# A planner that starts with its queue and two engines taken: one core, windowed attention into a softplus feed-forward

## The chip, the core and the metric

One core of one Trainium2 chip runs the kernel. The metric is the device time of one execution in microseconds (us). TensorE (PE) multiplies and loads its weights beside that (PEld), VectorE (DVE), ScalarE (ACT) and GpSimd (POOL) work on elements, SyncE (SP) issues the transfers, and the DMA engines carry them.

## The reference, cut to what matters

```python
scores = scale * np.matmul(q, k.transpose(0, 1, 3, 2))        # 8 x 8 heads, 576 x 64
mask_plain = (rel >= 0) & (rel < 32)                          # heads 0 to 3
mask_dil = (rel >= 0) & (rel < 128) & (rel % 4 == 0)          # heads 4 to 7
scores = np.where(masks, scores, -1e9)
attn = np.exp(scores - scores.max(-1))
attn = attn / (attn.sum(-1) + 1e-9)
x = np.matmul(attn, v)                                        # then 4608 tokens x 512
h = x @ w_in                                                  # 512 x 2048
g = np.maximum(h, 0.0) + np.log1p(np.exp(-np.abs(h)))
out = g @ w_out                                               # 2048 x 512
```

## The kernel before

The 4608 tokens are nine chunks of 512. All products are carried in high and low parts, so each product of a weight block is three matmuls of 512 columns (`xh`, `xl` and `parts`, `gh`, `gl`). Chunks 0 to 2 use the plain products: `h_ps` and `o_ps` are their sums in PSUM. Chunks 3 to 8 go in three pairs (`SUPERS`) through a scheme with seven products of sums of blocks instead of eight; its sums in PSUM are `x`, `y`, `z`, and `unit()` issues the matmuls of one product block. The sums of weight blocks that it needs (`w_b`, `w_t`) are worked out on DVE, ACT and POOL while the first chunks run, stored to DRAM (`keep_block` and `job`, 256 KB each) and fetched later into a ring of five buffers (`ring`).

Attention goes by couples of head groups. For each couple there are two "visits" of TensorE, which stand between the long matmuls: `scores` (`s_ps`) and `values` (`a_ps`). Behind the scores come the maximum and the exponentials, then `turn_squares`, a transpose on DVE that writes `sq`; four `turned<-sq` transfers of 64 KB write it to DRAM, and one `sq<-turned` of 256 KB fetches it back in the order that `values` needs. The values visit has two halves, one for each group of the couple (`a_ps<-v,sq` and `a_ps<-x_full,sq`), and each waits for a fetch of `sq`. Its results are normalized, turned, sent out (`rows<-x_full`) and fetched back (`x_full<-rows`) as the chunk's x.

All these transfers are issued by SP through `load_dma`, in one order. Each of the first 128 waits until the eighth before it has landed, so at most eight are under way.

What comes in which order is set in two ways. The start, up to about 98 us, is written out by hand (the string `OPENING`). All the rest is a list of tasks with costs and due times, which `planned()` puts in order when the kernel is built: for each engine it keeps when it is free, for the queue `queue_free`, and it takes the most urgent task that can begin. TensorE's own chain has a fixed order; only the visits are put in by the planner. `HURRIED` changes the urgency of tasks by their number, `CHOSEN` pins a task to one engine. The core of the planner is

```python
start = min(b for b, _ in begins)
if e == "SP":
    start = max(start, queue_free - BACKLOG)
_, at, n, t = min((not t.visit, urgency(t), t.n, t) for b, t in begins if b <= start)
...
if t.size:
    queue_free = max(queue_free, end) + t.size / DMA_RATE
    end = queue_free + DMA_LATENCY + t.size * DMA_EACH
```

At the end, `o_after()` adds the last sums of product 6 to `temp` and stores the last tiles (`out_t<-g_of`).

Of the kernel before, what the change touches and what calls it, by code (L numbers as in the profile page):

```python
# [18 lines left out]
ALU = mybir.AluOpType  # L19
# [5 lines left out]
P = 128  # L25
# [3 lines left out]
CH = 512  # L29
# [18 lines left out]
HALF = CH // 2  # L48
# [8 lines left out]
DEPTH = 8  # L57
THIN = 128
LAG = 2
HURRIED = {  # L60
# [6 lines left out]
}  # L67
CHOSEN = {
    295: "ACT", 467: "DVE", 535: "DVE", 554: "DVE", 586: "DVE", 595: "DVE", 819: "DVE", 853: "DVE", 865: "DVE",
    868: "DVE", 882: "DVE", 885: "DVE", 888: "DVE", 901: "DVE", 903: "DVE", 905: "ACT", 908: "DVE", 1210: "DVE",  # L70
    1213: "DVE", 1219: "DVE", 1238: "DVE", 1266: "DVE", 1281: "DVE", 1307: "DVE", 1322: "DVE", 1336: "DVE",
    1345: "DVE", 1580: "DVE", 1670: "DVE", 1676: "DVE", 1694: "DVE", 1716: "DVE", 1731: "DVE", 1767: "DVE",
    1772: "DVE", 1777: "DVE", 2010: "DVE", 2042: "DVE", 2094: "DVE", 2112: "DVE",
}
EXP_AND_LN = [t.name for t in act_sets.SETS].index("natural_log_exp_and_others")

# [38 lines left out]
def tile_windowed_attention_softplus_ffn(  # L115
# [47 lines left out]
    def load_dma(engine=None, **kw):  # L163
        ins = tc.keep_in_program_order((engine or nc.sync).dma_start(**kw))
        if held[0] is not None:
            tc.add_manual_dep(
                ins.ins,
                held[0].ins.name,
                mybir.DependencyInfo(mybir.DependencyClass.Sync, mybir.DependencyReason.DATA),
                reason="the load is held back until this matmul",  # L170
            )
            held[0] = None
        if engine is None and len(under_way) < THIN:
            if len(under_way) >= DEPTH:
                tc.add_manual_dep(
                    ins.ins,
                    under_way[-DEPTH].ins.name,
                    mybir.DependencyInfo(mybir.DependencyClass.Sync, mybir.DependencyReason.DATA),
                    reason="at most so many of the first loads under way",
                )  # L180
            under_way.append(ins)
# [740 lines left out]
    def transfer(run, *what, size, n=1, each=0.4, reads=(), writes=()):  # L922
        return Task("SP", each * n, lambda: run(*what), reads, writes, size=size)
# [52 lines left out]
    TILE = 2 * P * CH * 4  # L976
# [263 lines left out]
    BANKS = "xzyxyzy"  # L1240
# [8 lines left out]
    def bank_of(b, j):  # L1249
        if (b, j) not in banks:  # L1250
            n = "xyz".index(b)
            banks[b, j] = bank(f"{b}_{j}", "h" if b == "x" else f"o{2 * (n - 1) + j}")
        return banks[b, j]
# [16 lines left out]
    def unit(u):  # L1270
        _, i, k, jj = units[u]
        x, b = PRODUCTS[k][0], BANKS[k]
        begins = k < 3
        w = ring[u % RING]
        for n in range(2):
            dst, m = bank_of(b, n), 0
            for kk in range(2):
                for wp, xp in ((0, 0), (0, 1), (1, 0)):
                    if i == 0:
                        lhs, rhs = w[:, n, wp, kk * P : (kk + 1) * P], blocks[x][xp][:, kk]  # L1280
                        first, final = begins and m == 0, m == 5
                    else:
                        lhs, rhs = w[:, kk, wp, n * P : (n + 1) * P], moving[u % 3][xp][:, kk]
                        first, final = begins and jj == 0 and m == 0, jj == NCP - 1 and m == 5
                    matmul(out=dst, lhsT=lhs, rhs=rhs, start=first, stop=final, skip_group_check=not begins)
                    m += 1

    def evicted(k, j, dst, keys, t):
        b = BANKS[k]
        key = BANK_KEY[b][j]  # L1290
        if t is None:
            copy_task("ACT", 512, lambda: (dst()[:, j], banks[b, j]), reads=[key], writes=keys)
            return
        task(
            "DVE", 512, lambda: summed("DVE", dst()[:, j], banks[b, j], temps[t][:, j], ALU.add),
            reads=[key, (f"t{t}", j)], writes=keys,
        )
# [83 lines left out]
    def o_after(s, k):  # L1381
        first, second = SUPERS[s]
        to, t = ((0, None), (1, 0), (2, 0), ("a11", None), ("a22", 1), ("a12", 2), ("a21", 0))[k]
        if k == 3:
            half, c = 0, first
            n = next(turn_of_e) % 2
            keys, dst = both(f"e{n}"), lambda: spare[n]
        elif k > 3:
            half, c = ((1, second), (1, first), (0, second))[k - 4]
            name = {4: "a21", 5: "a11", 6: "a12"}[k]  # L1390
            keys, dst = g_keys(name, 1), lambda: g[name, 1]
        else:
            keys, dst = both(f"t{to}"), lambda: temps[to]
        for j in range(2):
            evicted(k, j, dst, [keys[j]], t)
            if k == 6 and s == len(SUPERS) - 1:
                rows = slice(j * P, (j + 1) * P)
                transfer(
                    lambda rows=rows, j=j: load_dma(out=out[rows, c * CH : (c + 1) * CH], in_=dst()[:, j]),
                    reads=[keys[j]], size=TILE // 2,  # L1400
                )
        if k > 2 and not (k == 6 and s == len(SUPERS) - 1):
            transfer(store, dst, half, c, reads=keys, size=TILE)

# [66 lines left out]
    def planned():  # L1471
        engines = ("PE", "POOL", "DVE", "ACT", "SP", "NONE")
        free, candidates = dict.fromkeys(engines, 0.0), {e: [] for e in engines}
        queue_free = port_free = seen = 0.0
        for t in reversed(tasks):
            for other in t.then:
                t.latest = min(t.latest, other.latest - t.tail())

        def offered(t):
            for e in t.options:  # L1480
                candidates[e].append(t)

        for t in tasks:
            if not t.left:
                offered(t)
        for _ in tasks:
            best = None
            for e in engines:
                begins = [
                    (max(free[e], t.ready, port_free if e in t.ports else 0.0, seen + APART if t.visit else 0.0), t)  # L1490
                    for t in candidates[e]
                ]
                if not begins:
                    continue
# [4 lines that stand above are left out]
                if best is None or (start, at, n) < best[:3]:  # L1499
                    best = start, at, n, t, e  # L1500
            start, _, _, t, e = best
            for other in t.options:
                candidates[other].remove(t)
            t.engine, t.begun, end = e, start, start + t.options[e]
            free[e] = end
            if t.visit:
                seen = end
            if e in t.ports:
                port_free = end
# [3 lines that stand above are left out]
            yield t  # L1513
            for other in t.then:
                lag = (
                    0.0 if e == other.main == "PE" else calm(other, end) if other.visit else 0.5 if other.main == "PE"
                    else 0.12 if other.main == e else 0.18
                )
                other.ready = max(other.ready, end + lag)
                other.left -= 1  # L1520
                if not other.left:
                    offered(other)
# [133 lines left out]
```

## Time and profile before

| | |
|---|---|
| Median of 3 runs | 817.3 us (816.92 to 817.5) |
| Profiled execution, device time | 819.88 us |
| Its span on the core | 818.1 us |
| TensorE busy | 801.9 us, 98% |
| DVE, ACT, POOL busy | 660.2, 501.8, 189.4 us |
| Moved by DMA | 218.94 MB, mean 268 GB/s |

The span is the time from the first to the last instruction on the core; the device time of the same execution is 1.8 us more. The profiled execution is 2.6 us over the median of the runs. Of the page's forty slices, TensorE's granted clock is below 0.9 in one alone, the second (0.6).

### The profile page before, as it was taken

The numbers are of one execution on the slowest core, as the hardware profiler recorded it, in microseconds if no ns is written. First come the engines' busy times: TensorE is split into PE (matmuls) and PEld (weight loads), VectorE is DVE, ScalarE is ACT, GpSimd is POOL, SyncE is SP. The second block draws the span as 40 slices with busy tenths as digits, with TensorE's granted clock in tenths as the row PEclk, the third lists the DMA queues.
The fourth block names the chain that finished last, engine by engine and source line by source line (L and its number), as shares of the span: only waits on it lengthen the run. The fifth ranks groups of instructions, "written<-read, shape, count | busy, mean of one in ns | idle before, by whom it ended". The sixth has DMA issues, their size and how long they took to land.

```text
span 818.1 us, 19668 instructions
## 1 busy us (share of the span) xinstructions
PE 801.9 (98%) x7833; PEld 654.2 (80%) x7835; DVE 660.2 (81%) x967; ACT 501.8 (61%) x1122; POOL 189.4 (23%) x132
## 2 busy tenths in 40 slices
PE   6999999999999999999999999999999999999998
PEld 4678888788888888888787888888888888888886
DVE  4798899957687766897999887897997846778974
ACT  5787788745666645596786413889943616775410
POOL 0000000054043324754313202202024302221510
PEclk9699999999999999999999999999999999999999
DMA  9774999968879673999988999879989675556573
GB/s 298 242 242 129 307 374 339 314 208 287 278 249 296 210 219 142 374 336 357 350 295 303 316 352 333 289 240 346 298 269 308 233 248 189 196 190 199 189 218 140
DMA packets 118490, 218.94 MB, mean 268 GB/s; under 512 B 11520, under 2 KB 53632, under 8 KB 118400
## 3 DMA queue, kind: packets, MB, share of 16 engines
q1 hardware_dynamic: 117968, 216.97, 79.1%
q8 instruction: 62, 1.02, 0.5%
q10 hardware_dynamic: 432, 0.72, 0.3%
q14 instruction: 28, 0.23, 0.1%
HBM read 162.07 MB, written 55.57 MB: 266 GB/s over the span
## 4 chain that ended last, share of the span: by engine, by line
PE 72%; DVE 10%; DMA 9%; ACT 5%; issue 2%; POOL 1%; SPq 0%; POOLq 0%; DVEq 0%; ACTq 0%
PE y L237 20%; PE z L237 12%; PE x L237 12%; PE h_ps L237 11%; PE o_ps L237 10%; PE a_ps L237 3%; DMA raw<-w 3%; PE s_ps L237 3%; DMA w_t<-cast 2%; ACT s L433 2%; ACT e L1308 1%; DVE g_of L940 1%; DVE a L216 1%; DMA v<-vp 1%; DMA k<-kdl 1%
## 5 line engine op out<-in xcount | busy, mean ns | idle before, releaser
L940 POOL TENSOR_TENSOR g_of<-g_of 128x1024 f32<-128x1024 f32 x33 | 80.3, 2434 | 258.6 <-DVE g_of L1311 133.3
L940 DVE TENSOR_TENSOR g<-g_of,g 128x1024 fp32r<-128x1024 f32 x84 | 121.3, 1450 | 15.0 <-ACT g L972 14.5
L237 PE MATMUL o_ps<-gh,parts 128*128 128x512 f32 x384 | 129.2, 394 | 0.0
L237 PE MATMUL h_ps<-xh,parts 128*128 128x512 f32 x384 | 129.1, 394 | 0.0
L972 ACT CAST g<-g_of 128x1024 fp32r<-128x1024 f32 x61 | 63.9, 1051 | 102.8 <-PE z L237 44.3
L1308 ACT ACTIVATE e<-e 128x1024 f32<-128x1024 f32 x96 | 101.1, 1058 | 1.7
L237 PE MATMUL y<-g,ring 128*128 128x512 f32 x432 | 100.5, 390 | 0.0
L237 PEld LDWEIGHTS y<-g,ring 128*128 128x128 f32 x432 | 80.8, 188 | 17.1
L940 POOL TENSOR_TENSOR b<-parts 128x512 f32<-128x512 f32 x29 | 40.4, 1393 | 213.5 <-DVE parts L231 143.8
L237 PEld LDWEIGHTS h_ps<-xh,parts 128*128 128x128 f32 x384 | 72.4, 188 | 15.6 <-DVE x_full L587 0.4
L237 PEld LDWEIGHTS o_ps<-gh,parts 128*128 128x128 f32 x384 | 72.1, 188 | 15.9
L433 ACT ACTIVATE s<-s,nm 128x64 f32<-128x64 f32 x224 | 74.8, 336 | 7.2 <-DVE nm L424 7.1
L237 PE MATMUL h_ps<-xl,parts 128*128 128x512 f32 x192 | 75.0, 391 | 0.0
L237 PE MATMUL o_ps<-gl,parts 128*128 128x512 f32 x192 | 74.8, 390 | 0.0
L237 PE MATMUL z<-g,ring 128*128 128x512 f32 x288 | 66.7, 390 | 0.5 <-DVE g L940 0.5
L237 PE MATMUL x<-g,ring 128*128 128x512 f32 x288 | 66.5, 390 | 0.0
L237 PE MATMUL z<-s_h,ring 128*128 128x512 f32 x192 | 63.3, 390 | 0.7 <-DVE temp L940 0.7
L237 PE MATMUL y<-s_h,ring 128*128 128x512 f32 x192 | 63.6, 392 | 0.3 <-DVE temp L940 0.3
L237 PEld LDWEIGHTS z<-g,ring 128*128 128x128 f32 x288 | 53.9, 188 | 12.1 <-DVE g L940 0.9
L237 PE MATMUL x<-a_h,ring 128*128 128x512 f32 x192 | 63.3, 390 | 0.0
L237 PEld LDWEIGHTS x<-g,ring 128*128 128x128 f32 x288 | 53.9, 188 | 11.5 <-DVE g L940 0.2
L940 DVE TENSOR_TENSOR g_of<-y,temp 128x512 f32<-128x512 f32 x60 | 39.6, 682 | 28.7 <-PE y L237 28.6
(111 smaller groups left out, 1522.4 us busy)
## 6 DMA issues: line engine op xcount, KB each, us to landing
ring<-w_t SPq DMA_DIRECT2D x96, 512.0 KB, 4.7
ring<-w_b SPq DMA_DIRECT2D x72, 512.0 KB, 5.1
raw<-w SPq DMA_DIRECT2D x64, 256.0 KB, 5.6
w_t<-cast SPq DMA_DIRECT2D x64, 256.0 KB, 5.5
w_b<-parts SPq DMA_DIRECT2D x48, 256.0 KB, 5.1
v<-vp SPq DMA_DIRECT2D x14, 512.0 KB, 5.7
x_full<-vp SPq DMA_DIRECT2D x14, 512.0 KB, 5.8
turned<-sq SPq DMA_DIRECT2D x112, 64.0 KB, 3.2
```

Of the source, the lines that this page charges most:

```text
L216: pin(nc.vector.scalar_tensor_tensor(out=ai, in0=low, scalar=29, in1=ai, op0=ALU.logical_shift_right, op1=ALU.bitwise_or,))
L237: last_matmul[0] = tc.keep_in_program_order(nc.tensor.matmul(**kw))
L433: pin(nc.scalar.activation(out=self.blocks[:, t], in_=src, func=AF.Exp, bias=self.nm[:, t : t + 1], scale=1.0 / 8.0 if self.masked else 1. ...
L940: pin((nc.gpsimd if name == "POOL" else nc.vector).tensor_tensor(out=dst, in0=a, in1=b, op=op))
L972: pin(nc.scalar.copy(out=dst, in_=src))
L1308: pin(nc.scalar.activation(out=to(), in_=of(), func=func, **kw))
```

## The change

The planner no longer starts from zero: the queue counts as taken for 14.5 us, DVE for 1.4 and ACT for 1.0, by what the opening left running. The tables `HURRIED` and `CHOSEN` are replaced by others that fit this. In the last unit of all, the matmuls of the second bank are done in two halves of 256 columns, and `o_after()` adds and stores that bank's tile in two halves.

```diff
+BEGUN = {"DVE": 1.4, "ACT": 1.0}
+QUEUE_BEGUN = 14.5
 HURRIED = {
-    18: -46, 57: -2, 80: 8, 81: -22, 173: -2, 179: -36, 180: -16, 183: 28, 198: -30, 295: 30, 338: -16, 554: -4,
...
+    0: -6, 7: 2, 20: -72, 24: -32, 40: -92, 50: -44, 57: -144, 63: -4, 65: -30, 76: -8, 86: -12, 93: -30,
...
-        for n in range(2):
-            dst, m = bank_of(b, n), 0
+        whole = [(n, slice(0, CH)) for n in range(2)]
+        for n, cols in whole if u < len(units) - 1 else [whole[0], (1, slice(0, HALF)), (1, slice(HALF, CH))]:
+            dst, m = bank_of(b, n)[:, cols], 0
...
-                        lhs, rhs = w[:, kk, wp, n * P : (n + 1) * P], moving[u % 3][xp][:, kk]
+                        lhs, rhs = w[:, kk, wp, n * P : (n + 1) * P], moving[u % 3][xp][:, kk, cols]
...
-            evicted(k, j, dst, [keys[j]], t)
             if k == 6 and s == len(SUPERS) - 1:
                 rows = slice(j * P, (j + 1) * P)
-                transfer(
-                    lambda rows=rows, j=j: load_dma(out=out[rows, c * CH : (c + 1) * CH], in_=dst()[:, j]),
-                    reads=[keys[j]], size=TILE // 2,
-                )
+                for n, cols in enumerate((slice(0, CH),) if j == 0 else (slice(0, HALF), slice(HALF, CH))):
+                    width = cols.stop - cols.start
+                    task(
+                        "DVE", width, lambda j=j, cols=cols: summed(
+                            "DVE", dst()[:, j, cols], banks[BANKS[k], j][:, cols], temps[t][:, j, cols], ALU.add
+                        ),
+                        reads=[BANK_KEY[BANKS[k]][j], (f"t{t}", j)], writes=[("last", j, n)],
+                    )
...
     def planned():
         engines = ("PE", "POOL", "DVE", "ACT", "SP", "NONE")
         free, candidates = dict.fromkeys(engines, 0.0), {e: [] for e in engines}
-        queue_free = port_free = seen = 0.0
+        free |= BEGUN
+        queue_free, port_free, seen = QUEUE_BEGUN, BEGUN["DVE"], 0.0
```

The opening's instructions stay as they are, and so does the order of the long matmuls. From about 98 us on, the order on all engines is another. DVE has 990 instructions instead of 967, ACT 839 instead of 837 (by the program's count), POOL 108 instead of 132, SP 718 transfers instead of 717. In the changed file the lines stand 13 further on (L237 becomes L250).

On SP, the first planned stretch, around the first two fetches of `sq`. Before, 35 blocks `w_b` stand between SP's first planned transfer and the first `turned<-sq`, and the piece around the fetches is

```order
L164 DMA w_b_3_1510<-parts 128x2x256
L164 DMA w_b_3_1522<-parts 128x2x256
L164 DMA x_full<-vp 128x1024
L164 DMA turned<-sq 32x4x128 x8
L164 DMA k<-kpl 128x544 x2
L164 DMA mask<-msk 128x512
L164 DMA w_b_3_1530<-parts 128x2x256
L164 DMA w_b_2_1537<-parts 128x2x256
L164 DMA sq<-turned 128x512
L164 DMA w_b_2_1549<-parts 128x2x256
L164 DMA w_b_2_1557<-parts 128x2x256
L164 DMA sq<-turned 128x512
```

and now, with 17 blocks ahead of the first `turned<-sq`,

```order
L177 DMA w_b_0_1547<-parts 128x2x256
L177 DMA turned<-sq 32x4x128 x4
L177 DMA x_full<-vp 128x1024
L177 DMA turned<-sq 32x4x128 x4
L177 DMA k<-kpl 128x544 x2
L177 DMA mask<-msk 128x512
L177 DMA w_b_2_1509<-parts 128x2x256
L177 DMA sq<-turned 128x512
L177 DMA w_b_2_1521<-parts 128x2x256
L177 DMA w_b_2_1529<-parts 128x2x256
L177 DMA w_b_0_1555<-parts 128x2x256
L177 DMA sq<-turned 128x512
```

Ahead of the second fetch stand 39 blocks `w_b` before and 21 now; the other transfers ahead of it are the same. Behind it, before the next couple's fetches, there are now 16 blocks `w_b` in a row, then `turned<-sq` x8, `kept`, two `w_b`, `v`, `rows` x4, `kept` and both fetches of `sq`.

On TensorE, the first planned values visit (`a_ps`). Before, it stands behind 530 long matmuls of 512 columns of the plain chunks:

```order
L237 MATMUL h_ps<-xh,parts 128x512
L237 MATMUL o_ps_2211<-gh,parts 128x512
L237 MATMUL o_ps_2211<-gl,parts 128x512
L237 MATMUL o_ps_2211<-gh,parts 128x512
L237 MATMUL a_ps<-v,sq 32x64 x32
L237 MATMUL a_ps<-x_full,sq 32x64 x32
L237 MATMUL o_ps_2220<-gh,parts 128x512
```

and now behind 458:

```order
L250 MATMUL h_ps<-xh,parts 128x512
L250 MATMUL o_ps_1400<-gh,parts 128x512
L250 MATMUL o_ps_1400<-gl,parts 128x512
L250 MATMUL o_ps_1400<-gh,parts 128x512
L250 MATMUL a_ps<-v,sq 32x64 x32
L250 MATMUL a_ps<-x_full,sq 32x64 x32
L250 MATMUL o_ps_1414<-gh,parts 128x512
```

The visit moves 72 long matmuls forward, the next values visit from 623 to 539 of them, so that 81 lie between the two instead of 93.

On DVE, the place that the kernel before reaches at about 400 us (`cast<-d` finishes a block for `w_t`; the additions into `temp` read the banks of `y` and `z` and so free them for TensorE). Before:

```order
L1311 SCALAR_TENSOR_TENSOR g_of<-g_of,e 128x1024
L1120 TENSOR_TENSOR cast<-d,cast 128x2x256
L940 TENSOR_TENSOR temp<-y_4589,temp 128x512
L940 TENSOR_TENSOR temp<-y_4596,temp 128x512
L940 TENSOR_TENSOR temp<-z_4568,temp 128x512
L419 SCALAR_TENSOR_TENSOR s<-s_ps,mask 128x512
L424 TENSOR_REDUCE nm<-s 128x8
L974 CAST g<-g_of 128x1024
L940 TENSOR_TENSOR temp<-z_4561,temp 128x512
```

Now:

```order
L1133 TENSOR_TENSOR cast<-b,cast 128x2x256
L1133 TENSOR_TENSOR cast<-d,cast 128x2x256
L953 TENSOR_TENSOR temp<-z_4566,temp 128x512
L953 TENSOR_TENSOR temp<-z_4573,temp 128x512
L953 TENSOR_TENSOR temp<-y_4590,temp 128x512
L953 TENSOR_TENSOR temp<-y_4597,temp 128x512
L987 CAST g<-g_of 128x1024
```

The two additions for `z` have come ahead of the two for `y`.

## Rows read from the trace of the kernel before

**Rows 1.** The page: engine table, and one group of weight loads (busy us, mean ns)
```profile
PE 801.9 (98%) x7833; PEld 654.2 (80%) x7835; DVE 660.2 (81%) x967; ACT 501.8 (61%) x1122; POOL 189.4 (23%) x132
...
L237 PEld LDWEIGHTS y<-g,ring 128*128 128x128 f32 x432 | 80.8, 188 | 17.1
```

**Rows 2.** TensorE's waits from 100 us on: total us, times, longest
```profile
PE a_ps L237 <- DVE a L207: 1.4, 1, 1.4
PE z L237 <- DVE temp L940: 0.7, 1, 0.7
PE z L237 <- DVE g L940: 0.5, 1, 0.5
PE y L237 <- DVE temp L940: 0.3, 1, 0.3
```

**Rows 3.** Timeline of TensorE around two values visits: start, duration, instruction, [idle before]
```profile
156.18 0.85 PE L237 MATMUL a_ps<-v,sq 64*32 64x64 f32 x64 [1.40 <-DVE a L207]
156.83 0.85 PE L237 MATMUL a_ps<-x_full,sq 64*32 64x64 f32 x64
157.60 0.50 PE L237 MATMUL o_ps<-gh,parts 128*128 128x512 f32 x1
157.94 0.39 PE L237 MATMUL o_ps<-gl,parts 128*128 128x512 f32 x1
...
178.61 0.39 PE L237 MATMUL h_ps<-xh,parts 128*128 128x512 f32 x1
178.93 0.80 PE L237 MATMUL a_ps<-v,sq 64*32 64x64 f32 x60
```

**Rows 4.** Timeline of SP's transfers, 109.8 to 152.4 us: start, us until the last issue
```profile
109.92 1.02 SPq L164 DMA_DIRECT2D x_full<-qp  x2
...
112.14 9.59 SPq L164 DMA_DIRECT2D w_b<-parts  x12
...
123.22 18.48 SPq L164 DMA_DIRECT2D w_b<-parts  x23
...
142.55 4.39 SPq L164 DMA_DIRECT2D turned<-sq  x8
...
151.85 0.51 SPq L164 DMA_DIRECT2D sq<-turned  x1
```

**Rows 5.** Windows: busy us of each engine, PEclk, DMA share, GB/s
```profile
114.40:156.10 41.70, 40.38 (x299) 32.99 (x297) 41.46 (x81) 34.91 (x95) 1.42 (x1) 1.00 1.00 335
110.00:128.00 18.00, 18.00 (x81) 14.92 (x80) 17.93 (x35) 16.25 (x41) 0.00 (x0) 1.00 1.04 363
128.00:147.00 19.00, 19.00 (x206) 15.62 (x205) 18.97 (x39) 16.08 (x40) 0.00 (x0) 1.00 0.99 325
157.00:179.00 22.00, 22.00 (x167) 17.97 (x161) 15.70 (x25) 12.84 (x34) 10.35 (x11) 1.00 0.85 267
...
380.00:410.00 30.00, 28.98 (x305) 23.04 (x306) 26.24 (x43) 20.97 (x42) 11.59 (x9) 1.00 1.00 352
```

**Rows 6.** Timeline of DVE, 128 to 143 us: the first `sq` transpose
```profile
132.34 0.66 DVE L475 STREAM_TRANSPOSE sq<-s 128x512 f32<-128x512 f32 x1
```

**Rows 7.** Timeline of ACT, 395 to 404 us
```profile
400.71 0.62 ACT L972 CAST cast<-d 128x512 fp32r<-128x512 f32 x1 [1.64 <-DMA w_t<-cast]
```

**Rows 8.** Timeline of DVE, 396 to 408 us
```profile
401.98 1.28 DVE L940 TENSOR_TENSOR temp<-y,temp 128x512 f32<-128x512 f32 x2
```

**Rows 9.** Timeline of TensorE, 400 to 410 us
```profile
402.71 0.50 PE L237 MATMUL y<-s_h,ring 128*128 128x512 f32 x1 [0.32 <-DVE temp L940]
...
406.43 0.50 PE L237 MATMUL z<-s_h,ring 128*128 128x512 f32 x1 [0.70 <-DVE temp L940]
```

**Rows 10.** Timeline of all engines, 805 to 819 us: the last addition
```profile
814.20 0.69 DVE L940 TENSOR_TENSOR g_of<-y,temp 128x512 f32<-128x512 f32 x1 [0.67 <-PE y L237]
```

**Rows 11.** DVE by line and form: an operation on 256 columns (busy us, mean ns)
```profile
L620 DVE TENSOR_TENSOR xl<-a_ps,xh 128x256 fp32r<-128x256 f32 x8 | 3.0, 417 | 0.7 <-ACT xh L616 0.7
```

**Rows 12.** Timeline of TensorE, 44 to 45 us: four transposes of 128 columns
```profile
44.48 0.60 PE L464 MATMUL t_ps<-opened,s 128*128 128x128 f32 x4
```

More of the change, by code (lines that the diff above doesn't have):

```diff
@@ L59 @@
 LAG = 2
+BEGUN = {"DVE": 1.4, "ACT": 1.0}
+QUEUE_BEGUN = 14.5
 HURRIED = {
[6 rows of a table removed]
[14 rows of a table added]
 }
 CHOSEN = {
[L69 to L73, printed above, removed]
+    285: "DVE", 292: "ACT", 314: "DVE", 323: "DVE", 324: "DVE", 325: "DVE", 326: "DVE", 535: "DVE", 536: "DVE",
+    537: "DVE", 544: "DVE", 560: "DVE", 564: "DVE", 577: "DVE", 593: "DVE", 594: "DVE", 595: "DVE", 796: "ACT",
+    819: "DVE", 822: "DVE", 827: "DVE", 829: "DVE", 852: "DVE", 853: "DVE", 871: "DVE", 873: "DVE", 875: "DVE",
+    882: "DVE", 883: "DVE", 885: "DVE", 898: "DVE", 901: "DVE", 903: "DVE", 908: "DVE", 1079: "ACT",
+    1210: "DVE", 1216: "DVE", 1224: "DVE", 1266: "DVE", 1281: "DVE", 1292: "ACT", 1296: "ACT", 1307: "DVE",
+    1312: "DVE", 1322: "DVE", 1335: "DVE", 1345: "DVE", 1584: "ACT", 1625: "DVE", 1670: "DVE", 1731: "DVE",
+    1741: "DVE", 1748: "DVE", 1772: "DVE", 1777: "DVE", 1782: "DVE", 1783: "ACT", 1790: "DVE", 1795: "DVE",
+    1800: "DVE", 1805: "DVE", 2010: "DVE", 2034: "DVE", 2063: "DVE", 2104: "DVE",
 }
@@ L1394, in o_after @@
         for j in range(2):
-            evicted(k, j, dst, [keys[j]], t)
             if k == 6 and s == len(SUPERS) - 1:
                 rows = slice(j * P, (j + 1) * P)
-                transfer(
-                    lambda rows=rows, j=j: load_dma(out=out[rows, c * CH : (c + 1) * CH], in_=dst()[:, j]),
-                    reads=[keys[j]], size=TILE // 2,
-                )
+                for n, cols in enumerate((slice(0, CH),) if j == 0 else (slice(0, HALF), slice(HALF, CH))):
[6 more added lines that the diff above has]
+                    )
+                    transfer(
+                        lambda rows=rows, j=j, cols=cols: load_dma(
+                            out=out[rows, c * CH + cols.start : c * CH + cols.stop], in_=dst()[:, j, cols]
+                        ),
+                        reads=[("last", j, n)], size=width * P * 4,
+                    )
+                continue
+            evicted(k, j, dst, [keys[j]], t)
         if k > 2 and not (k == 6 and s == len(SUPERS) - 1):
```

18 rows, old and new, of the table HURRIED are left out of this document.

## The prediction

> **What bounds the kernel now.** I read the page's engine table first. TensorE is busy for 801.9 us of a span of 818.1 us [rows 1], so almost nothing can be won except where it stands idle, and everything that makes it stand costs the full time. The profiled execution took 819.88 us, 2.6 us more than the median of the three runs (817.3 us). The sum below is made on its trace and then added to the median.
>
> The list of TensorE's waits from 100 us on is next [rows 2]. The opening, up to about 98 us, is issued as before, so its waits stay. Behind it are only four: 1.40 us before an `a_ps` visit, and 0.3, 0.7 and 0.5 us before `y` and `z`. Together they are 2.9 us: this is all that a better order can win, apart from the last few microseconds of the kernel.
>
> The largest one must be understood. The timeline of TensorE [rows 3] shows a values visit that starts at 156.18 after 1.40 us of nothing. The row puts the wait down to a DVE instruction `a` that has no link to the visit. The program makes the visit wait for its two `sq` fetches, and the second of these was issued by SP at 151.85 [rows 4], 4.33 us before the visit started. For a transfer of 256 KB in a full queue that is what one expects, so I take the fetch for the cause. And why was it issued so late? SP's timeline shows one unbroken row of issues: twelve `w_b` blocks took 9.59 us, the next 23 took 18.48 us, which is 0.80 us a block both times. The windows [rows 5] say why: over 114.4 to 156.1 us the DMA engines were busy for a share of 1.00 at 335 GB/s. **SP's place in line is the clock of this stretch: what stands ahead of a fetch decides when it lands.** The `sq` transposes which feed it ran at 132.34 and soon after [rows 6], ten microseconds before SP came to `turned<-sq` at 142.55.
>
> The Trainium skill, "DMA: Bandwidth & Descriptors", section "Specifications", gives about 358 GB/s as the limit of HBM for one core. The rows of this case (335 over the whole stretch, 363 at best) agree.
>
> **The change, part by part.**
>
> *The first values visit.* Two things move, and they move by different amounts. On TensorE the visit stands after 458 of the long 512-column matmuls instead of 530, so 72 fewer. Such matmuls follow each other by 0.227 us: from the one at 157.94 to the one at 178.61 [rows 3] there are 91 steps in 20.67 us. 72 of them are 16.35 us, so TensorE is at the visit at 154.78 - 16.35 = 138.43 us (154.78 is the start less the wait of 1.40). Its second half starts 0.65 us behind the first (156.18 to 156.83), which is 139.08. On SP the second `sq` fetch has 21 `w_b` blocks ahead of it from 109.9 us on, instead of 39; all other transfers ahead of it are the same ones (two `k` loads, two of queries, two of `v`, eight `turned`, two more of `k`, a mask, the first `sq`). So it is issued 18 x 0.803 = 14.45 us earlier, at 137.40, and its data are there 4.33 us later, at 141.73. TensorE gains 16.35 us on its place and the queue only 14.45. The second half waits 141.73 - 139.08 = **2.65 us**, and the old 1.40 us go. Bounds: at 363 GB/s, the fastest window [rows 5], the 27.5 us from 109.92 to 137.40 would shrink in the ratio 335/363 to 25.4, and the wait to 0.5; if the queue stays at 317 to 325 GB/s, as it did where `turned` was written, it grows to about 3.5.
>
> *The second values visit* (the other couple of the same chunk). Between the two visits TensorE has 81 long matmuls, where it had 93. From the start of the second half of the first visit it is there after 0.77 (156.83 to 157.60) + 0.34 + 80 x 0.227 + 0.32 us = 19.6, at 161.3. SP carries, behind the second `sq` of the first couple and up to the first `sq` of this one: 18 `w_b`, eight `turned` of a quarter block, two `kept`, a `v` of two blocks, four `rows` of half a block, and that `sq`: 27 blocks of 256 KB. At 0.803 us they take 21.7, to 163.4. So it waits **2.1 us**. The second estimate comes from the old chain: from 157.60, where the first visit ended, to 178.93, where the second began with its data just there, are 21.33 us; the same chain from 142.50 ends at 163.8 and gives 2.5. That chain was not held by the queue alone, since the window 157 to 179 shows only 267 GB/s, and so the wait can also be 0. I take 2.1 and keep 0 to 2.5.
>
> *Around 400 us.* The queue is full again (352 GB/s, share 1.00 [rows 5]). ACT's `cast<-d` waited 1.64 us for a store of `w_t` [rows 7], DVE came to the additions into `temp` only at 401.98 [rows 8], and TensorE waited 0.32 for `y` and 0.70 for `z` [rows 9]. In the new order the four additions behind that `cast<-d` are `z`, `z`, `y`, `y` instead of `y`, `y`, `z`, and then the other `z` after three more rows. Thus `y` comes two additions later, about 1.2 us (a pair took 1.28 from the start of one to the end of the other [rows 8], and they overlap a little), and the wait for `z` disappears: +1.2 - 0.7 = +0.5. Half of it I strike off, as the block itself may be earlier by a little: **+0.2**, bounds -1.5 (all three waits gone) and +1.5.
>
> *The end.* The last addition (DVE 814.20, 0.69 us [rows 10]) becomes two of 256 columns, 0.42 each [rows 11], the first of which lies beside the matmuls. That takes off 0.27. The last store has half the bytes; I give that nothing to 0.3. The six last matmuls become twelve of 256 columns. Their number of columns is the same. Weight loads double to twelve at 188 ns [rows 1], 2.26 us if one could not begin before the last had ended, against 1.36 us of matmuls: that would cost 0.9. But four transposes of 128 columns, each with a weight load of its own, took 0.60 us together [rows 12], less than four such loads in a row (0.75), so loads overlap and the halves cost about 0.05 to 0.1. SP issues one more store, but a smaller one. Sum of the end: **-0.3**, bounds -0.6 and +0.7.
>
> *Everything else*: the other visits stay within 12 to 70 long matmuls of their old places and none of them waited before; POOL gets 24 instructions less and DVE 23 more, in stretches where DVE's work lies beside TensorE's. I set them at nothing. If DVE becomes late, the additions that free `y` and `z` are next to be waited for.
>
> Sum: -1.40 + 2.65 + 2.1 + 0.2 - 0.3 = +3.25 us. The profiled execution would take 823.1, the median **820.5 us**.
>
> **The rivals.**
>
> *The queue keeps up.* If the new mix of transfers runs 10% faster than 335 GB/s, both fetches land in time: 24.7 us instead of 27.5 for the first. The old 1.40 goes and the end gives 0.3: 815.6 us, and 814.1 if the waits around 400 go as well (they hang on the same queue). For it: 363 GB/s in 110 to 128 us. Against it: that pace held for 18 us only, and 325 followed with a share of 0.99. The Trainium skill, "DMA: Bandwidth & Descriptors", section "Bandwidth", measured 425 GB/s at 16 MB; at that figure the queue would be ahead of TensorE everywhere, and no window here has shown it for a single stretch. Chance 0.15.
>
> *The waits only change places.* The first visit waits 1.0 to 1.5 us instead of 1.40, and the second finds its data there, because its chain is shorter by the `w_b` and `x_full` transfers that stood between its two fetches. That is 817.0 with the end's gain. For it: the lower bounds above, both reached by a queue only 5% faster. Chance 0.16.
>
> *The blocks themselves are late.* DVE was busy 17.93 of 18 us and 18.97 of 19 [rows 5] while it decodes weights; if the earlier visits' softmax pushes the blocks back, SP, which issues in order, stands at a `w_b` that isn't ready, and the `sq` fetch behind it with it. Three DVE instructions late (0.6 us each) at both places are some 3 us more: 823.5. It decides as soon as SP shows a wait on DVE ahead of the first `turned`. Chance 0.12.
>
> *The halves cost.* Weight loads that do not overlap: 820.5 + 0.3 + 0.7 = 821.5. Chance 0.02.
>
> **How the numbers follow.** The forecast has 0.55, with a range of its own from 818.9 to 822.5. 0.2% is 1.6 us, about what a measurement of this kernel can tell from no change. Faster: the first rival and a little of the second, 0.17. Same: most of the second and the lower edge of the forecast, 0.15. Slower: the rest, 0.68. The range that should hold 8 in 10 takes the forecast, the second rival and the nearer part of the first and the third: 815.4 to 823.4.
>
> **What would show it.** Right: TensorE idle in the middle of the first visit near 139 to 142 us, and before the second near 161 to 164, each ended by an `sq` fetch; SP without a gap and the DMA share at 0.97 to 1.00 there; a wait for `y` near 406 and none for `z`. Wrong: both visits start without a wait; or SP idle in 110 to 140 with a wait on DVE. The end is right if the last DVE row has about 0.42 us and the span ends less than 3.9 us behind the start of the last addition (now 818.1 - 814.2). What would upset the sum most is a queue that moves `w_b` blocks in under 0.75 us.

## The result, and the profile after

The changed kernel takes 824.23 us (median of 6, 823.2 to 825.97) against 817.11 us for the kernel before (median of 6): a ratio of 1.0086, 95% interval 1.0066 to 1.0107, which is +7.0 us (5.4 to 8.7). Slower, as forecast, but by twice as much: the forecast was 820.5, its range ended at 823.4.

TensorE's waits from 98 us on in the profile after (total us, times, longest):

```profile
PE a_ps L250 <- issue: 2.4, 1, 2.4
PE a_ps L250 <- DMA sq<-turned: 2.4, 2, 1.8
PE y L250 <- DVE temp L953: 2.3, 1, 2.3
PE o_ps L250 <- issue: 0.5, 1, 0.5
PE s_ps L250 <- issue: 0.3, 1, 0.3
```

There were 2.9 us of them [rows 2], now there are 7.9. The timeline of TensorE shows where they stand around the first two planned values visits:

```profile
136.32 0.39 PE L250 MATMUL o_ps<-gh,parts 128*128 128x512 f32 x1
137.26 0.85 PE L250 MATMUL a_ps<-v,sq 64*32 64x64 f32 x64 [0.54 <-DMA sq<-turned]
139.96 0.85 PE L250 MATMUL a_ps<-x_full,sq 64*32 64x64 f32 x64 [1.85 <-DMA sq<-turned]
...
142.20 0.40 PE L250 MATMUL o_ps<-gh,parts 128*128 128x512 f32 x1 [0.50 <-issue]
...
159.70 0.39 PE L250 MATMUL o_ps<-gh,parts 128*128 128x512 f32 x1
162.53 1.12 PE L250 MATMUL a_ps<-v,sq 64*32 64x64 f32 x61 [2.44 <-issue]
...
164.50 0.79 PE L250 MATMUL h_ps<-xh,parts 128*128 128x512 f32 x1
165.09 0.63 PE L250 MATMUL h_ps<-xl,parts 128*128 128x512 f32 x1
165.52 0.72 PE L250 MATMUL h_ps<-xh,parts 128*128 128x512 f32 x2
```

The first visit waits in both halves, the second before its start: the places of the forecast. The row of the second names no releaser (`issue`), but it is the fetch too: the first couple's second fetch, issued at 134.56, took 5.3 us to land, and its half starts at 139.96; the next couple's first fetch was issued at 158.62, took 3.8 us, and the second visit starts at 162.53. Behind the second wait something stands that the forecast did not have: the halves of the visit take 1.12 us where one took 0.80 [rows 3], and the next long matmuls start 0.59 and 0.43 us apart instead of 0.34 and 0.227. The windows (busy us of each engine, PEclk, DMA share, GB/s) say why: the granted clock is at the lower of its two levels, 1.2 GHz, for some 3 us.

```profile
160.00:162.50 2.50, 0.09 (x1) 0.01 (x1) 2.50 (x6) 2.34 (x4) 0.00 (x0) 0.96 1.06 335
162.50:163.50 1.00, 0.97 (x73) 1.00 (x77) 0.57 (x1) 0.00 (x0) 0.95 (x1) 0.50 0.99 152
163.50:165.00 1.50, 1.50 (x79) 1.33 (x64) 0.39 (x1) 0.00 (x0) 0.70 (x1) 0.50 0.75 253
165.00:166.00 1.00, 1.00 (x4) 0.77 (x3) 1.00 (x3) 0.00 (x0) 0.00 (x0) 0.64 1.04 384
...
114.40:156.10 41.70, 38.80 (x413) 31.62 (x412) 37.99 (x78) 33.96 (x94) 0.00 (x0) 1.00 1.00 332
```

The last of these rows answers to the first of [rows 5]: 332 GB/s at a share of 1.00, so the queue is as full as before. SP's timeline (start, us until the last issue) answers to [rows 4]:

```profile
107.77 1.00 SPq L177 DMA_DIRECT2D k<-kdl  x2
...
111.92 13.19 SPq L177 DMA_DIRECT2D w_b<-parts  x17
125.20 2.33 SPq L177 DMA_DIRECT2D turned<-sq  x4
...
134.56 1.05 SPq L177 DMA_DIRECT2D sq<-turned  x1
135.65 12.31 SPq L177 DMA_DIRECT2D w_b<-parts  x16
148.09 4.55 SPq L177 DMA_DIRECT2D turned<-sq  x8
```

From SP's first planned transfer to the second fetch are 26.8 us (forecast: 27.5, from 109.92 to 137.40). The third place is near 406 us; the rows are those of ACT, DVE and TensorE, one view each:

```profile
405.50 0.62 ACT L985 CAST cast<-d 128x512 fp32r<-128x512 f32 x1 [3.99 <-DMA w_t<-cast]
```

```profile
406.15 0.69 DVE L1133 TENSOR_TENSOR cast<-d,cast 128x512 fp32r<-128x512 f32 x1 [3.42 <-ACT cast L985]
406.76 1.28 DVE L953 TENSOR_TENSOR temp<-z,temp 128x512 f32<-128x512 f32 x2
407.96 1.28 DVE L953 TENSOR_TENSOR temp<-y,temp 128x512 f32<-128x512 f32 x2
```

```profile
408.69 0.50 PE L250 MATMUL y<-s_h,ring 128*128 128x512 f32 x1 [2.31 <-DVE temp L953]
```

ACT waits for the store of `w_t` for 3.99 us (1.64 in [rows 7]), DVE for ACT, TensorE for DVE. And the end, all engines:

```profile
817.13 0.69 DVE L953 TENSOR_TENSOR g_of<-y,temp 128x512 f32<-128x512 f32 x1 [4.49 <-PE y L250]
818.56 0.76 DVE L953 TENSOR_TENSOR g_of<-y,temp 128x256 f32<-128x256 f32 x2 [0.74 <-PE y L250]
```

Both halves of the last addition stand behind the last matmul, which starts at 818.24; none lies beside it.

The two spans differ by 4.1 us only (822.2 and 818.1), for the openings of the two executions differ as well, with the same instructions: over 16 to 33 us the granted clock was 0.51 in the profile before and 0.90 in the one after. The first planned scores visit starts at 101.73 before and at 100.00 after; from there to the last matmul's start are 712.05 and 718.24 us. So **the planned part became 6.2 us longer**; this is the number to explain. (Up to the start of the last addition but one, which the halves don't touch, it is 6.0 us; up to the end of the span 5.8, as the span ends 4.0 us behind the last matmul's start instead of 4.3.) The clock of the opening alone does not set when it ends: two of the kernels below, the one with the last bank whole and the one with the first visit alone later, had 0.70 over the same stretch and came to that visit at 99.67 and at 101.10.

### The profile page after: what moved, and what is told of

It reads as the page before. It is cut to its first block, busy times and chain, and to the rows that moved or that the text cites. A ratio compares the mean times of both kernels' runs of the same rounds, so it can differ in the third digit from the quotient of the medians.

```text
span 822.2 us, 19653 instructions
## 1 busy us (share of the span) xinstructions
PE 798.2 (97%) x7839; PEld 652.3 (79%) x7841; DVE 662.7 (81%) x990; ACT 501.4 (61%) x1124; POOL 152.3 (19%) x108
## 4 chain that ended last, share of the span: by engine, by line
PE 91%; DMA 5%; DVE 1%; issue 1%; ACT 1%; SPq 0%; POOL 0%; DVEq 0%; ACTq 0%; POOLq 0%
PE y L250 23%; PE o_ps L250 16%; PE z L250 15%; PE x L250 15%; PE h_ps L250 15%; PE a_ps L250 3%; PE s_ps L250 3%; DMA raw<-w 2%; DMA w_t<-cast 2%; DMA k<-kdl 1%; DMA sq<-turned 1%; DMA x_full<-vp 0%; SPq L177 0%; PE t_ps L477 0%; DVE temp L953 0%
## 5 line engine op out<-in xcount | busy, mean ns | idle before, releaser
L250 PE MATMUL o_ps<-gh,parts 128*128 128x512 f32 x384 | 129.3, 394 | 0.5 <-issue 0.5
L250 PE MATMUL h_ps<-xh,parts 128*128 128x512 f32 x384 | 129.5, 395 | 0.0
L985 ACT CAST g<-g_of 128x1024 fp32r<-128x1024 f32 x57 | 59.6, 1049 | 114.6 <-PE y L250 41.0
L953 DVE TENSOR_TENSOR g<-g_of,g 128x1024 fp32r<-128x1024 f32 x84 | 115.1, 1374 | 17.1 <-ACT g L985 16.6
L953 POOL TENSOR_TENSOR g_of<-g_of 128x1024 f32<-128x1024 f32 x26 | 63.4, 2438 | 219.8 <-DVE g_of L1325 112.3
L250 PE MATMUL y<-g,ring 128*128 128x512 f32 (+1 forms) x438 | 100.4, 387 | 0.0
L250 PEld LDWEIGHTS y<-g,ring 128*128 128x128 f32 x438 | 81.3, 188 | 16.9
L250 PEld LDWEIGHTS h_ps<-xh,parts 128*128 128x128 f32 x384 | 72.7, 189 | 15.5 <-DVE e L702 0.2
L250 PEld LDWEIGHTS o_ps<-gh,parts 128*128 128x128 f32 x384 | 72.1, 188 | 15.8
L250 PE MATMUL h_ps<-xl,parts 128*128 128x512 f32 x192 | 75.3, 392 | 0.0
L250 PE MATMUL o_ps<-gl,parts 128*128 128x512 f32 x192 | 74.8, 390 | 0.0
L953 POOL TENSOR_TENSOR b<-parts 128x512 f32<-128x512 f32 x21 | 29.6, 1413 | 231.1 <-DVE parts L244 157.5
L250 PE MATMUL x<-g,ring 128*128 128x512 f32 x288 | 66.8, 391 | 0.0
L250 PE MATMUL z<-g,ring 128*128 128x512 f32 x288 | 66.6, 390 | 0.0
L250 PE MATMUL y<-s_h,ring 128*128 128x512 f32 x192 | 63.5, 392 | 2.3 <-DVE temp L953 2.3
L250 PE MATMUL x<-a_h,ring 128*128 128x512 f32 x192 | 63.3, 391 | 0.0
L250 PE MATMUL z<-s_h,ring 128*128 128x512 f32 x192 | 63.3, 391 | 0.0
L250 PEld LDWEIGHTS x<-g,ring 128*128 128x128 f32 x288 | 53.8, 188 | 11.7 <-DVE g L953 0.3
L953 DVE TENSOR_TENSOR g_of<-y,temp 128x512 f32<-128x512 f32 (+1 forms) x61 | 39.8, 672 | 28.8 <-PE y L250 28.8
L250 PEld LDWEIGHTS z<-g,ring 128*128 128x128 f32 x288 | 54.0, 188 | 11.2
```

The lines of the kernel that those rows point to most:

```text
L250: last_matmul[0] = tc.keep_in_program_order(nc.tensor.matmul(**kw))
L953: pin((nc.gpsimd if name == "POOL" else nc.vector).tensor_tensor(out=dst, in0=a, in1=b, op=op))
L985: pin(nc.scalar.copy(out=dst, in_=src))
```

## The experiments

All kernels compute the whole reference. Most take the changed kernel's finished plan and hold back some tasks, with whatever needs them, until a given task has been issued:

```diff
+    plan = held_back(list(planned()), held, until)
-    for t in planned():
+    for t in plan:
```

Times are medians beside the kernel before on the same chip; the latter came out at 817.6 to 819.3 us in the four jobs. So kernels of different jobs are compared by their ratios to it: 0.001 is 0.8 us, and the changed kernel, which was timed in a job of its own, has 1.0086.

**Both visits later.** `held_back({200}, 304)` and `({217}, 365)`: the two values visits.

> The changed kernel, with its first two planned values visits put later among the long matmuls (21 and 24 of them later), and what needs their results behind them; SP's order is as it was. Theory A, the queue is the clock: the fetches of sq land when the queue comes to them, whatever TensorE does (139.8 and 162.4 us in the changed kernel's trace). The first visit then finds its data (0.54 + 1.85 + 0.50 us of waiting go), TensorE comes to the second at about 162.3, so at most 0.2 us are left of 2.44, and the clock does not fall behind it: about -6.5 us against the changed kernel, 817.7. Theory B, a fixed chain of 21.7 us runs from the end of the first visit to the second one's data (140.7 to 162.4): the first visit now ends at about 142.9, the second waits until 164.6, 2.3 us with the fallen clock behind it, and only the first waits go: 821.1. Theory C, the waits have nothing to do with where the visits stand: 824.

Measured: 818.66 us, ratio 1.0010 (0.9988 to 1.0031). The first visit has no wait, the second 0.74 us, the clock stays at 1.00 behind it. Theory A, nearly to the number; B's 2.3 us are not there.

**Eight blocks behind the fetches.** `held_back({123, ..., 130}, 216)`; 216 is the fourth fetch of `sq`.

> The changed kernel, with 8 of the 17 blocks w_b that stand on SP ahead of the first turned<-sq stored behind the last of the four fetches of sq instead; visits as in the changed kernel. Theory A, the queue is the clock: 8 blocks at 0.80 us are 6.4 us, so the fetches land at about 133.4 and 156.0; TensorE wants them at 137.9 and (without the first waits) at about 156.8. Both waits go and the clock stays up: about -6.5 us against the changed kernel, 817.7. Theory B, a fixed chain of 21.7 us from the end of the first visit: the first waits go, the visit ends at 137.6, the second gets its data at 159.3 and waits 2.5 us: 821.1. Theory C, something else ends the waits, as the profile's word 'issue' for the second would have it: 824.

Measured: 818.12 us, ratio 1.0003 (0.9985 to 1.0022). The visits in its timeline:

```profile
136.19 0.86 PE L250 MATMUL a_ps<-v,sq 64*32 64x64 f32 x64
...
157.70 0.81 PE L250 MATMUL a_ps<-v,sq 64*32 64x64 f32 x62 [1.41 <-issue]
```

The first wait is gone. The second is 1.41, between A (none) and B (2.5). With the visits where they were and SP's order changed, the time falls as far as with SP's order kept and the visits moved: it is the distance between the two that costs. By the ratios the two kernels win 6.8 and 6.2 of the 7.0 us.

**The order of the additions.** `held_back({1172, 1173}, 1177)`: `z` behind `y`.

> The changed kernel, with the two additions for y ahead of the two for z on DVE at the place near 407 us, and nothing else. If the order of the additions made the wait for y longer, y is free two additions (1.2 us) sooner, the wait of 2.31 us becomes about 1.1, and z, which TensorE needs 2.7 us after y, is not waited for: 823.0. If all of that wait is the late cast<-d (ACT idle 3.99 us behind a store of w_t), the wait stays at 2.3 and the time at 824.2.

Measured: 824.77 us, ratio 1.0078 (1.0053 to 1.0103). The wait for `y` falls to 1.5 us, but `x` then waits 1.1 us for a `g` that was not waited for before. Nothing is won that shows: the wait became shorter, if less than expected (1.1), and the expectation overlooked what is late next.

**The last bank whole again**, and **only the halves**, put into the kernel before:

```diff
-        for n, cols in whole if u < len(units) - 1 else [whole[0], (1, slice(0, HALF)), (1, slice(HALF, CH))]:
+        for n, cols in whole:
```

> The changed kernel without the halves: the last bank's matmuls, addition and store whole again. As forecast, the halves give 0.3 us: from the last matmul's start to the end of the span 4.3 us instead of 4.0, and 824.5. If the halves only cost (weight loads that don't overlap), the twelve matmuls' place takes 0.9 us less and the time is 823.3.

> The kernel before with only the last bank in halves (matmuls of 256 columns, two additions, two stores); tables and planner as before. About 0.3 us less: 816.8. If weight loads don't overlap, 0.6 more: 817.7. Neither can be told from 817.1 by the times; the rows of the end tell.

Measured: 825.4 us, ratio 1.0084 (1.0056 to 1.0112), and 819.94 us, ratio 1.0023 (1.0001 to 1.0045). The times don't tell; the rows do. The end of the whole kernel, and then of the one with only the halves:

```profile
817.73 0.69 DVE L953 TENSOR_TENSOR g_of<-y,temp 128x512 f32<-128x512 f32 x1 [4.49 <-PE y L250]
819.09 0.69 DVE L953 TENSOR_TENSOR g_of<-y,temp 128x512 f32<-128x512 f32 x1 [0.67 <-PE y L250]
```

```profile
812.60 0.69 DVE L942 TENSOR_TENSOR g_of<-y,temp 128x512 f32<-128x512 f32 x1 [4.49 <-PE y L239]
814.03 0.76 DVE L942 TENSOR_TENSOR g_of<-y,temp 128x256 f32<-128x256 f32 x2 [0.74 <-PE y L239]
```

From the start of the last addition but one to the end of the last are 2.05 us whole (819.09 + 0.69 - 817.73) and 2.19 in halves, here as in the changed kernel. From there to the end of the span are 3.2 us in the kernel before and in the one with only the halves, 2.9 in the changed kernel and in the one with the whole bank, so the smaller store gives nothing that shows, and the expected 4.3 against 4.0 us is a difference between the two plans and not of the halves. The halves cost 0.14 us. By the ratio the kernel with only the halves is 1.9 us over the kernel before, just clear of its interval; 0.14 us don't explain that, and it stays open. In its profile the opening was 1.1 us quicker than in the profile before, and its first values visit waited 2.3 us instead of 1.40: TensorE came sooner, the fetch did not.

**Three blocks behind the second fetch, in the kernel before.** `held_back({155, 156, 157}, 182)`.

> The kernel before, with three of the blocks w_b that stand ahead of its first turned<-sq stored right behind the second fetch of sq; visits as before. Theory A, the fetch was what the visit at 156.18 waited for: it lands 2.4 us sooner, 0.9 us before TensorE is there, and the 1.40 us go. The next visit (178.93, data just there): if its data come by a chain from the first visit's end, they come 1.4 us sooner too, and the time is 815.7; if they come by the queue alone, whose bytes up to there are the same, that visit waits 1.3 us and the time stays 817.1. If the DVE instruction that the profile names was the cause, the wait of 1.40 stays and the time is 817.1.

Measured: 817.25 us, ratio 0.9990 (0.9973 to 1.0007): too small to time, but the visit that waited 1.40 us starts at 154.01 with no wait, and the list of waits shows none at the next one either; the wait for `y` near 400 us grew from 0.3 to 0.8 us. So the fetch was the cause, not the DVE instruction that the row named.

```profile
154.01 0.86 PE L237 MATMUL a_ps<-v,sq 64*32 64x64 f32 x64
```

**The starting values at zero**, with the new tables (`QUEUE_BEGUN = 0.0`, `BEGUN` zero).

> The changed kernel with the planner starting from zero again (queue, DVE and ACT free) and the new tables kept. The first values visit then stands 21 long matmuls earlier than in the changed kernel, and the second fetch of sq behind 39 blocks w_b instead of 21. Theory A, the queue is the clock: TensorE is there 4.8 us earlier and the data 14.5 us later, so it waits some 22 us instead of 2.4; the second visit, with all blocks stored by then, waits less than before. About +18 us against the changed kernel, 842, and more if the clock falls. If the visits' waits are not set by SP's order, the time stays within 2 us of 824.

Measured: 834.79 us, ratio 1.0206 (1.0178 to 1.0235). Slower by some 10 us than the changed kernel, not 18: the wait stands one step earlier than expected.

```profile
PE s_ps L250 <- DMA k<-kdl: 12.2, 1, 12.2
...
PE a_ps L250 <- DMA sq<-turned: 1.3, 1, 1.3
```

The scores visit already waits 12.2 us for its `k` loads, which now stand behind blocks, and this gives the fetches time. So with the new tables the starting values are worth some 10 us. The old tables with the starting values were not run; which of the two parts of the change brought visit and fetch out of step is therefore not separated.

**A planner with the measured rate**: `DMA_RATE` 0.326e6 for 0.38e6, tables as changed.

> The changed kernel, whose planner reckons with a queue of 326 KB a millisecond in thousands (0.326e6 bytes a us, the 0.80 us a block of the trace) instead of 0.38e6; tables and starting values as changed. The first values visit then stands behind 3 more long matmuls and its second fetch behind 16 blocks instead of 21; the second visit stands 36 long matmuls later. Theory A: both waits go, -6.5 us. What the rest of the plan does with tables that were searched for the other rate is open: I take 0 to +4 us for it; 818 to 822. If the planner's rate is not what put the visits too early, they wait as in the changed kernel: 824 or more.

Measured: 828.23 us, ratio 1.0132 (1.0092 to 1.0171), outside what was expected. The values visits no longer wait, which fits a planner that had reckoned with 380 GB/s where the trace has 332, but TensorE waits 3.6 us for `s_l` near 331 us and 2.2 us at two scores visits. Tables searched at one rate do not serve at another; whether tables searched at this rate would, is not tried.

**The 16 blocks between the couples behind**, with the first visit as it was, and **the first visit alone later**.

> The changed kernel, with the 16 blocks w_b that stand on SP between the first couple's fetches of sq and the second couple's turned<-sq stored behind the second couple's fetches instead; all else, the first visit's waits too, as it was. Theory A, the second visit's data come late because SP is behind those 16 blocks (12.3 us of issues in the changed kernel's trace): SP comes to turned<-sq as soon as DVE's transposes are done (about 142 us), the fetches are issued by about 151 and land by 155, before TensorE is there at 159.9; the wait of 2.44 us and the fallen clock behind it (0.6 us) go: 821.1. Theory B, the chain from the end of the first visit takes its 21.7 us whatever SP carries: 824.2.

> The changed kernel, with the first planned values visit alone put 21 long matmuls later; the second stays where it was. Theory A, the queue is the clock: the first waits (3.1 us) go, TensorE is at the second visit 3.1 us sooner, at 156.8, its data land at 162.4 as before, and it waits 5.6 us: nothing is won, 824.2, or a little more where the clock stays low for longer. If each visit's wait is its own affair: 821.1. If the second visit hangs on the end of the first by a fixed chain: the data land at 164.6, and the time is 826.

Measured: 824.01 us, ratio 1.0060 (1.0037 to 1.0084), and 825.77 us, ratio 1.0088 (1.0067 to 1.0110). In the first the second visit has no wait at all:

```profile
141.25 0.85 PE L250 MATMUL a_ps<-x_full,sq 64*32 64x64 f32 x64 [2.06 <-DMA sq<-turned]
162.23 0.80 PE L250 MATMUL a_ps<-v,sq 64*32 64x64 f32 x60
```

So SP's order makes that wait, as A says. By the ratios only 2.1 us are won against the changed kernel, where 3.1 were expected, and the two intervals overlap: in this profile the first visit's waits were longer (2.9 us together), the clock was at 0.58 over 142 to 146 us behind them, and the wait for `y` was 2.1 us, with a lower clock behind it too. In the second the wait is not removed but handed on:

```profile
142.54 0.86 PE L250 MATMUL a_ps<-v,sq 64*32 64x64 f32 x64
...
165.65 1.13 PE L250 MATMUL a_ps<-v,sq 64*32 64x64 f32 x61 [7.77 <-DMA sq<-turned]
```

7.8 us are more than A's 5.6. But in this execution SP came to its first planned transfer only at 110.67 us instead of 107.77, and it took 3.80 us over the three blocks ahead of the first couple's second fetch (1.88 in the changed kernel), both ahead of the visit that was moved. The second couple's first fetch was then issued at 161.96 instead of 158.62. So most of the difference came with the queue and not by the visit. By the ratio the kernel is as slow as the changed one (1.0088 and 1.0086): nothing is won, as A says; the 826 of the fixed chain lies within the spread, so the time alone does not decide between them.

**All blocks behind** (the eight and the sixteen).

> The changed kernel with both groups of blocks (8 ahead of the first turned<-sq, 16 between the two couples) stored behind the second couple's fetches, visits where they stood. If the queue's order makes both waits, and what was given back when only the second wait went was the clock that fell behind the first, no wait of 0.5 us or more is left before 170 us, the clock stays full there, and the whole 6 to 7 us go: 817.5. If what was given back lies in the moved blocks themselves (the later fetches stand behind them), this kernel gives it back too: 820 or more.

Measured: 820.24 us, ratio 1.0013 (0.9994 to 1.0033). No wait is left before 170 us. But `h_ps` now waits 1.2 us for DVE near 180 us, a scores visit 1.1 near 360, and `y` 3.0 us near 403, with the clock at 0.50 behind it. By the ratio 6.0 us are won against the changed kernel. That lies between the two expectations; whether the moved blocks make the new waits is not shown.

**Near 400 us.** `held_back({905}, 1163)` puts `cast<-d` behind the additions; the next kernel has that, both visits later and the last bank whole; the third is the kernel before with its three blocks behind and `({972, 1238}, 1172)`, `({906}, 1177)`.

> The changed kernel, with the block that waits for a store near 405 us (cast<-d on ACT and its second half on DVE) put behind the two additions for z and the two for y. If the late cast<-d is what TensorE's wait of 2.31 us for y comes from, the additions run when TensorE has left the banks, that wait goes and the time is 821.9, less if the late block does not make another wait. If the wait only moves (the stores and the ring's loads behind them are late as well), the time stays within 1 us of 824.2.

> The changed kernel with the two visits later (21 and 24 long matmuls), cast<-d behind the additions, and the last bank whole again. If the three waits are each what the trace shows, they add up: the visits' alone came out at 818.7, its wait of 3.02 us for y and the low clock behind it (1.3 us) go too: 814.5, under the kernel before (817 to 818). If the late store takes back what cast<-d gives, 818.

> The kernel before, with three blocks w_b behind the second fetch of sq (0.8 us less when done alone), and near 400 us the second half of cast<-d behind the two additions for y, and the other addition for z ahead of a maximum and a cast. If the waits before y and z (0.32 and 0.70 us) come from DVE's order, they go: 815.5. If the ring's loads, which stand in the same full queue, are late as well, the waits stay under another name, and it is 816.8.

Measured: 823.39 us, ratio 1.0060 (1.0038 to 1.0082), which is 2.1 us under the changed kernel by the ratios, about the 2.3 of the first expectation, with intervals that overlap; 817.95 us, ratio 0.9987 (0.9966 to 1.0007); and 817.73 us, ratio 0.9979 (0.9961 to 0.9997). The waits of the first, second and third:

```profile
...
PE z L250 <- DVE g L953: 0.7, 1, 0.7
PE y L250 <- DMA ring<-w_t: 0.5, 1, 0.5
...
```

```profile
PE a_ps L250 <- issue: 2.4, 1, 2.4
PE y L250 <- DMA ring<-w_t: 0.5, 1, 0.5
...
```

```profile
PE a_ps L237 <- DMA sq<-turned: 2.1, 2, 1.6
PE z L237 <- DVE g L940: 0.5, 1, 0.5
```

The wait for the additions is gone in all three. In the first two the ring's load takes 0.5 us of it back; in the third, made from the kernel before, nothing is left near 400 us, and the 0.5 us before `z` stand near 432.

In the second kernel the three gains do not add up to 814.5: the wait of 2.4 us is the second values visit again, which waited 0.74 with the same two visits moved. Its fetch was issued at 161.00 us, 1.5 us later than there.

The third is the only one here that is faster than the kernel before beyond its interval (by 0.03% at the least, 0.2% in the middle). One such interval among fourteen can be chance. Its second values visit waits 1.6 us, and one near 277 us 0.5; the kernel with the three blocks alone has neither wait, though its plan is the same up to there. What the first visit wins is thus given back in one execution and not in the other.

## Why the prediction came out short

The direction, the two visits and their cause are shown: moving either the visits or SP's blocks takes some 6 us off (from a ratio of 1.0086 to 1.0010 and 1.0003). What failed is the sum of the terms beside the visits: the clock behind a wait was put at nothing (+1.1 us), the place near 400 us at +0.2 (+0.8), the end at -0.3 (+0.14), and "everything else" at nothing (+0.8 for two short waits). By rows, the 6.2 us of the planned part:

| | forecast | measured |
|---|---|---|
| the old wait | -1.40 | -1.40 |
| first visit | +2.65 | 0.54 + 1.85 = +2.39 |
| `o_ps` behind it | 0 | +0.50 |
| second visit | +2.1 | +2.44 |
| clock behind it | 0 | +1.1 |
| near 400 us | +0.2 | 2.31 - 0.32 - 0.70 - 0.5 = +0.8 |
| scores visit | 0 | +0.3 |
| end | -0.3 | +0.14 |
| sum | +3.25 | +6.3 |

- **The visits.** "TensorE gains 16.35 us on its place and the queue only 14.45" held: the first visit's wait to 0.26 us, the second's to 0.34. Part of that is luck. The second fetch was issued 0.7 us sooner behind SP's first planned transfer than forecast (26.8 us for 27.5, at 0.77 to 0.78 us a block), and its data were used 5.40 us behind the issue (134.56 to 139.96) instead of 4.33; the two misses nearly cancel. The size is no accident of one execution: three other kernels here have the same plan up to these visits (the order of the additions, the last bank whole, `cast<-d` behind), and in their profiles the visits and the `o_ps` behind them wait 4.9 to 5.4 us in all; here it is 5.3. The wait of `o_ps` is not the visit's own: the kernel with the planner's rate measured has a like wait of 0.9 us there and none at the visit. What it waits for stays open.
- **The clock.** The forecast took what lies behind a wait as unchanged. From the visit's start to its first long matmul are 1.97 us instead of 1.41 (178.93 to 180.34 in the trace before), and the next three matmuls lose 0.25, 0.20 and 0.10: 1.1 us. This is the largest term that was left out. It varies with the execution: in the kernel with the other order of the additions the same visit waited 2.41 us and the clock stayed at 1.00.
- **Near 400 us.** "`y` comes two additions later" names the smaller part. The late store is the larger: ACT's idle time before `cast<-d` grew by 2.35 us. Putting the order back took 0.8 us off the wait for `y`; putting the late block behind the additions took it away.
- **The end.** "The first of which lies beside the matmuls" failed. The first half's addition starts at 818.56, 0.32 us behind the start of the last of all twelve matmuls, and the second half's follows it without a wait. Why the first half is not released sooner is not tested; the twelve matmuls go to one bank, and both additions name that bank as what they read.
- **From the trace to the median.** The sum was made on an execution whose opening ran at half clock for 17 us, and then added to the median as if every execution had that opening. By medians the step is +7.0. To the start of the last addition but one, the planned part is 711.1 and 712.0 us in the two profiles that have the plan of before (the kernel before, and the one with only the halves), and 717.1 and 718.1 in the two that have the changed plan (the changed kernel, and the one with the whole bank): 5.1 to 6.9 us more. The rest lies within the interval, and the runs don't settle it.
- **The rivals.** The blocks were not late: SP waited 0.8 us for DVE in all, in two waits, over 107 to 126 us. The queue did not keep up: 332 GB/s around the visits. The Trainium skill ("DMA: Bandwidth & Descriptors") gives 425 GB/s measured at 16 MB ("Bandwidth") and about 358 as the limit for one core ("Specifications"). This stretch stays under both. But 358 is no limit in this case, as the prediction took it to be: the kernel before moved 416 GB/s over 406 to 410 us and the changed one 409 over 400 to 406. Nor are both lower bounds "reached by a queue only 5% faster": the 0.5 us at the first visit belong to 363 GB/s, which is 8% more than 335.

## What to carry to other kernels

Where a queue is full, the place of a fetch in it decides when its data come. When a planner moves a consumer and its fetch, compare the two shifts, in matmuls times their step and in transfers times theirs, before anything else. A wait that is moved is not a wait that is gone: taking one away made another wait appear or grow in six of these kernels. And a wait of one profile is known only to a us or two: the same plan, run again, showed the same visit with 1.1 to 2.4 us of waiting, and the clock behind it fell or stayed. A tile stored in halves helps only if its first half can be worked on while the second is still being made; here it was not.

## What was not expected of the hardware

The granted clock fell to 0.50 behind the wait of 2.44 us at the second visit, for about 3 us; behind the wait of 2.31 us for `y` in the same trace it stayed at 1.00. In the run with the whole last bank it was 0.50 over 138.8 to 145.6 us, from the first visit's first wait on. Twice it stayed at 1.00 behind a wait of the same length at the same second visit; the rows are from the kernel with the other order of the additions and from the one with both visits later, `cast<-d` behind and the whole bank:

```profile
163.38 0.80 PE L250 MATMUL a_ps<-v,sq 64*32 64x64 f32 x61 [2.41 <-issue]
```

```profile
164.94 0.80 PE L250 MATMUL a_ps<-v,sq 64*32 64x64 f32 x61 [2.43 <-issue]
```

So the length of the wait alone does not tell whether the clock falls. The same opening ran 16 to 33 us at 0.51 in one execution and 0.90 in another, and ended 1.7 us apart.
